# The mask and the query decay tables of a retention + two-layer FFN kernel made on the chip from small tables, with the second weight words loaded later and two decoding steps moved behind one sum

## The chip, the cores and the metric

One core of one Trainium2 chip runs the whole program. The metric is the device time of one execution in microseconds (us), median of three runs. The engines are TensorE (PE, its weight loads are PEld), VectorE (DVE), ScalarE (ACT), GpSimd (POOL) and SyncE (SP, which here only issues DMAs). Each takes its own instructions strictly in program order and waits where an operand, or a buffer that it will overwrite, is not free.

## The reference

Retention (attention with a decay per head and no softmax), then two feed-forward layers over the same 2304 tokens:

```python
scores = scale * np.matmul(q, k.transpose(0, 1, 3, 2))      # q, k, v: 4 x 8 x 576 x 64
gamma = 1.0 - 2.0 ** (-5.0 - np.arange(H, dtype=np.float32))
rel = pos[:, None] - pos[None, :]
Dmat = np.where(rel >= 0, gamma[:, None, None] ** rel[None, :, :], 0.0)
x = np.matmul(scores * Dmat[None], v)                       # -> 2304 x 512
h = x @ w_in;  x = np.maximum(0.01 * h, h) @ w_out          # 512 -> 2048 -> 512
h = x @ moe2_w_in;  h = np.maximum(h, 0.0);  return (h * h) @ moe2_w_out
```

The inputs q, k, v are float32. The weights are float64 and reach the chip as pairs of 32-bit words.

## The kernel before

**Retention** runs over 20 chunks (4 batches, each of four chunks of 128 tokens and one of 64; chunks 4, 9, 14 and 19 are the short ones). In the text chunk i has these steps: s_i (`scores`, L541) multiplies queries and keys of the chunk on PE; r_i (L544, L546) multiplies the scores by the mask on DVE; `decay` multiplies q (L555) and one half of k's heads (L559) by decay tables on POOL, `decay_rest` (L567) the other half of k's heads on ACT; out_i (L581, L590) forms the chunk's output on PE, which ACT copies out (L593); sums_i (L599) adds the chunk to the running state, which ACT copies (L603). The table `gq[0]` holds the query decays of the second chunk of a batch; those of later chunks are scaled copies of it (`make_gq`, L492). Scores go to two wide PSUM buffers by turns, so s_i needs r_(i-2) done. Loads are issued by SP in the order of the code: six buffers for q and k, four for the rows of k and v.

**Decoding.** Each weight pair of words ("raw") is turned into two float32r parts by steps on ACT and DVE. `steps_in` makes seven combinations of the first matrix (L153 on ACT, then L163 to L183 on DVE, L189 on ACT, L191 on DVE); `steps_out` does the second matrix (L153, L204, L206, L208, L210, L212 on DVE, L215 on ACT, L217, L220 on DVE). `run(n, limit)` writes the next n steps at the place in program order where it is called. The first pair of words lands in a part of `ysb[2]`, all later ones in one staging buffer, `raw`.

**The layers** hold eight groups of four blocks of 128 hidden units (`g`), and in each group three parts of 768 tokens (`p`). `first` runs seven products (Strassen-like, L321) into two PSUM buffers `a` and `b` by turns: A11, A12, S2, S3, S1, A22, S4. Between them DVE forms sums; the one of this text is L390, which reads `a` after product S1 and has to be done before product S4 writes `a` again. `second` (L425) has two halves t = 0, 1; in layer 0 each half fills four accumulators (e = 0 to 3), which share four PSUM banks with those of the other half, in layer 1 three accumulators take the four banks by turns. In group 0 ACT copies each finished accumulator out (L434). While group 0 of a layer works on a part, `operands` prepares the next part (L260 on ACT; L264, L274, L276, L279, L285 on DVE). `pace` is called between the products and accumulators with a running count `now`; `run` in it writes up to two decoding steps, except at counts 6 and 8 of each part's 15.

The order of every engine is the order in which the code is written; nothing reorders it.

Of the kernel before, what the change touches and what calls it, by code (L numbers as in the profile page):

```python
# [19 lines left out]
P = 128  # L20
# [32 lines left out]
@with_exitstack  # L53
def retention_ffn_kernel(ctx: ExitStack, tc: tile.TileContext, full, rows, half, halfv, w1, w2, const, mask, gk, out):

# [399 lines left out]
    class Retention:  # L455
# [27 lines left out]

        def load_gq(self):
            nc.sync.dma_start(self.gq[0].rearrange("p a t -> p (a t)"), const)

        def make_gq(self, c):

            if 1 < c <= FULL:
                to = self.gq[c - 1]  # L490
                for a in range(NP):
                    nc.scalar.activation(to[:, a], self.gq[0][:, a, : to.shape[2]], AF.Copy, scale=self.step[:, c - 2, a : a + 1])  # L492

        def load_mask(self):
            nc.sync.dma_start(self.mask.rearrange("p j a t -> p (j a t)"), mask)

# [136 lines left out]
    with tc.manual_schedule():  # L633
        with tc.tile_pool(name="att", bufs=1) as pool, tc.tile_pool(name="outputs", bufs=1, space=PSUM) as outputs:
            att.append(Retention(pool, outputs))
            ret = att[0]
            n = len(chunks)
            ret.load(0)
            weights.ahead()
            ret.load_mask()  # L640
            ret.load_gk()
            ret.load_rows(0)
            ret.load(1)
            ret.load_gq()
            ret.load(2)
# [4 lines left out]
            ret.open_table()  # L650
            ret.keep_warm(WARM[0])
            ret.scores(0)
            ret.decay(0)
            run(FIRST, GROUP)
            ret.decay_rest(0)
            scored = 1
            for i in range(n):
                if i + DEEP < n:
                    ret.load(i + DEEP)
                if i + ROWS < n:  # L660
                    ret.load_rows(i + ROWS)
                if i == 1 or weights.loads < GRP and weights.free:
                    weights.free = False
                    weights.ahead()
# [5 lines left out]
                ret.keep_warm(WARM[i + 1] if i + 1 < len(WARM) else 0)  # L670
                ret.output(i)
                ret.make_gq(i + 2)
                if i + 1 < n:
# [37 lines left out]
        for layer in range(2):  # L711
            for g in range(NG):
# [6 lines left out]
                def pace(now, ceiling):  # L719

                    into = min(1, (now - 15 * p) / (6 if busy[p] else 12 if p == NB - 1 else 15))
                    share = (0, *SHARE.get(i, (0.36, 0.71)), 1)
                    part = share[p] + (share[p + 1] - share[p]) * into
                    want = start + math.ceil((limit - start) * part)

                    while len(kept) > LAG:
                        store(*kept.pop(0))
                    while builds and now >= built[0] and build():
                        built[0] = max(built[0], now - 1) + SPACE
                    if not builds:  # L730
                        while kept:
                            store(*kept.pop(0))
                    weights.clock = whole * i + now
                    if now % 15 not in (6, 8):
                        run(min(2, max(want, start if now > 1 else 0) - done[0]), ceiling)
# [27 lines left out]
def constants():  # L763

    gamma = (1.0 - 2.0 ** (-5.0 - np.arange(H, dtype=np.float32))).astype(np.float64)
    scale = 1 / np.sqrt(D)
    row, col = np.arange(P)[:, None], np.arange(C)[None, :]
    gq = gamma[row // D + 2 * (col // P)] ** (P + col % P) * scale
    pair = np.arange(NP)[None, :]
    step = [gamma[row // D + 2 * pair] ** (c * P) for c in range(1, FULL)]  # L770
    since = col % P - row
    mask = [np.where(since >= 0, gamma[2 * (col // P) + j] ** np.maximum(since, 0) * scale, 0) for j in range(2)]
    gk = gamma ** -(np.arange(FULL)[:, None] * P + row[:, :, None]).astype(np.float64)
    return [a.astype(np.float32) for a in (gq, np.concatenate(mask, axis=1), np.concatenate([gk.reshape(P, -1), *step], axis=1))]

# [46 lines left out]
```

## Time and profile before

| | |
|---|---|
| median of 3 runs | 825.92 us (825.62 to 826.03) |
| the profiled execution | 826.09 us, its span 824.3 us |
| granted TensorE clock | 1.00 of full speed over the span |
| PE busy | 810.1 us, 98% of the span |
| DVE busy | 594.0 us, 72% |
| ACT busy | 352.3 us, 43% |
| POOL busy | 37.5 us, 5%, all of it in the first 75 us |

The times in the sections below are microseconds from the start of the span; the execution's own time is 1.8 us longer than the span. "Idle" is time of an engine just before an instruction; the name behind "<-" is what ended it.

### The profile page before, as it was taken

The page shows a single profiled execution, that of the slowest core. Times are in us where ns is not written, and L with a number is a line of the kernel's source. Part 1 is how long each engine was busy: PE and PEld are TensorE (multiplying, and loading weights), DVE is VectorE, ACT ScalarE, POOL GpSimd, SP SyncE. Part 2 cuts the span into 40 slices and gives each one's busy share as a digit, 9 for nine tenths or more (in the row PEclk, how much of TensorE's full clock was granted, in tenths as well). Part 3 has the DMA queues.
Part 4 walks back from the last instruction along what each step waited for, and adds up shares of the span by engine and source line. Part 5 has one row for each costly group of instructions (what it writes and reads, how often), then busy time and mean ns, then how long its engine had stood idle before and what let it go on. Part 6 is the DMA issues. An engine that isn't in the chain of part 4 may idle for free.

```text
span 824.3 us, 12698 instructions
## 1 busy us (share of the span) xinstructions
PE 810.1 (98%) x5216; PEld 765.3 (93%) x5216; DVE 594.0 (72%) x734; ACT 352.3 (43%) x511; POOL 37.5 (5%) x36
## 2 busy tenths in 40 slices
PE   7999999999999999999999999999999999999998
PEld 7788999999999999999999888998998998998996
DVE  5798887766665766667668989878876877853644
ACT  4777666453342452352444556443323333311211
POOL 3563000000000000000000000000000000000000
PEclk9999999999999999999999999999999999999999
DMA  9997549874773665665715437964864845744712
GB/s 349 395 362 295 219 148 361 342 286 134 293 254 139 246 253 178 259 228 193 269 52 230 165 155 270 397 234 150 312 224 155 308 173 205 263 171 179 289 51 76
DMA packets 45130, 190.91 MB, mean 232 GB/s; under 512 B 5136, under 2 KB 6160, under 8 KB 45072
## 3 DMA queue, kind: packets, MB, share of 16 engines
q1 hardware_dynamic: 44784, 189.31, 61.8%
q8 instruction: 41, 0.67, 0.3%
q10 hardware_dynamic: 288, 0.79, 0.3%
q14 instruction: 17, 0.14, 0.0%
HBM read 152.33 MB, written 37.75 MB: 231 GB/s over the span
## 4 chain that ended last, share of the span: by engine, by line
PE 86%; DVE 5%; DMA 4%; ACT 2%; issue 1%; SPq 0%; ACTq 0%; DVEq 0%
PE yps L425 45%; PE a L321 22%; PE b L321 16%; DMA kv<-in_rows 3%; DMA raw<-in_w 1%; PE ops L590 1%; PE scps L541 1%; DMA ysb<-in_w 1%; ACT sf L153 1%; PE ops L581 1%; DVE ilo L191 0%; ACT t L333 0%; PE sums L599 0%; DVE t L376 0%; DVE sf L167 0%
## 5 line engine op out<-in xcount | busy, mean ns | idle before, releaser
L321 PE MATMUL a<-x,ihi 128*128 128x384 f32 x768 | 195.9, 335 | 2.3 <-DVE t L390 2.3
L321 PE MATMUL b<-x,ihi 128*128 128x384 f32 x568 | 144.3, 334 | 0.0
L321 PEld LDWEIGHTS a<-x,ihi 128*128 128x128 f32 x768 | 138.6, 188 | 4.6 <-DVE t L390 3.5
L425 PE MATMUL yps<-ghi,ohi 128*128 128x384 f32 x384 | 128.6, 335 | 0.4 <-ACT ysb L434 0.4
L321 PE MATMUL a<-x,ilo 128*128 128x384 f32 x384 | 128.5, 335 | 0.0
L425 PE MATMUL yps<-glo,ohi 128*128 128x384 f32 x384 | 128.3, 334 | 0.0
L425 PE MATMUL yps<-ghi,olo 128*128 128x384 f32 x384 | 128.3, 334 | 0.0
L362 DVE TENSOR_TENSOR glo<-t,ghi 128x768 fp32r<-128x768 f32 x96 | 91.7, 955 | 45.9 <-ACT ghi L357 45.4
L436 DVE TENSOR_TENSOR ysb<-yps,ysb 128x384 f32<-128x384 f32 (+1 forms) x126 | 75.9, 610 | 61.9 <-PE yps L425 61.6
L425 PE MATMUL yps<-ohi,glo 128*128 128x512 f32 x288 | 112.3, 390 | 0.0
L425 PE MATMUL yps<-olo,ghi 128*128 128x512 f32 x288 | 112.3, 390 | 0.0
L425 PE MATMUL yps<-ohi,ghi 128*128 128x512 f32 x288 | 112.0, 389 | 0.0
L357 ACT ACTIVATE ghi<-t 128x768 fp32r<-128x768 f32 x96 | 81.1, 845 | 68.2 <-DVE t L335 54.8
L350 ACT ACTIVATE s<-a 128x768 f32<-128x768 f32 x47 | 38.2, 813 | 154.7 <-PE a L321 154.7
L321 PEld LDWEIGHTS b<-x,ihi 128*128 128x128 f32 x568 | 102.5, 188 | 0.4 <-ACT s L350 0.3
L321 PE MATMUL b<-x,ilo 128*128 128x384 f32 x284 | 94.9, 334 | 0.0
L425 PEld LDWEIGHTS yps<-ghi,ohi 128*128 128x128 f32 x384 | 72.1, 188 | 1.3 <-ACT ysb L434 0.7
L425 PEld LDWEIGHTS yps<-ghi,olo 128*128 128x128 f32 x384 | 72.1, 188 | 0.0
L425 PEld LDWEIGHTS yps<-glo,ohi 128*128 128x128 f32 x384 | 72.1, 188 | 0.0
L321 PEld LDWEIGHTS a<-x,ilo 128*128 128x128 f32 x384 | 72.1, 188 | 0.0
L425 PEld LDWEIGHTS yps<-ohi,glo 128*128 128x128 f32 x288 | 54.0, 188 | 11.3
L425 PEld LDWEIGHTS yps<-olo,ghi 128*128 128x128 f32 x288 | 54.0, 188 | 11.0
(77 smaller groups left out, 981.4 us busy)
## 6 DMA issues: line engine op xcount, KB each, us to landing
x<-x SPq DMA_DIRECT2D x168, 768.0 KB, 6.0
raw<-in_w SPq DMA_DIRECT2D x62, 512.0 KB, 5.7
kv<-in_rows SPq DMA_DIRECT2D x16, 512.0 KB, 6.6
out<-ysb SPq DMA_DIRECT2D x18, 256.0 KB, 2.0
q<-in_full SPq DMA_DIRECT2D x16, 256.0 KB, 6.5
kt<-in_full SPq DMA_DIRECT2D x15, 256.0 KB, 6.0
kv<-in_halfv SPq DMA_DIRECT2D x4, 256.0 KB, 6.5
ysb<-in_w ACTq DMA_DIRECT2D x1, 512.0 KB, 6.5
```

What stands on the lines that cost most here:

```text
L153: nc.scalar.activation(f32(a), f32(raw[:, :, 1]), AF.Abs)
L321: nc.tensor.matmul(ps[:, u, :HT], a[:, w, s], x[:, b, k], start=(start and k == 0 and i == 0), stop=(k == 1 and i == 2), skip_group_check= ...
L350: nc.scalar.activation(t, ps[:, :, :HT], AF.Copy)
L357: nc.scalar.activation(h, t, AF.Copy)
L362: nc.vector.tensor_tensor(l, t, f32(gs[key][0]), sub)
L425: nc.tensor.matmul(acc, a, b, start=(j == u == i == 0), stop=(j == 1 and u == NU - 1 and i == 2))
L436: nc.vector.tensor_tensor(y, acc, y, add)
L541: nc.tensor.matmul(o, k[s, c], q[s, c], start=True, stop=True, skip_group_check=True)
L581: nc.tensor.matmul(o, self.state[s, a], q[s, a * n : (a + 1) * n], start=(p == 0), stop=False, skip_group_check=True)
L590: nc.tensor.matmul(o, kv[f, 1, s], r, start=(c == 0 and p == 0), stop=(p == NP - 2), skip_group_check=True)
```

## The change

Three things change.

**Tables.** The mask (128 x 1024 float32, 512 KB) and the first query table (128 x 512, 256 KB) are no longer loaded. A table of 8 x 1792 float32 (57 KB: per head the powers of gamma, going down along the keys and up along the queries, and a selector of heads) and a causal table of 128 x 128 zeros and ones (64 KB) are loaded instead, into a part of `ysb[1]`. Two PE products over 8 rows give the powers of all heads; DVE multiplies them by the causal table into the mask. A third product gives the query table, which ACT copies out of PSUM. That product's PSUM bank is the one in which `keep_warm` writes.

**Loads.** The second pair of words is issued in iteration 2 of the chunk loop instead of iteration 1. The scores of chunk 1 and their mask are written directly behind out_0, ahead of two decoding steps.

**Pace.** At count 4 of a part no decoding steps are written where a group 0 works on a part that prepares the next one, except for the very first: that is part 1 of layer 0, and parts 0 and 1 of layer 1. The steps come later in the same part.

```diff
+        def load_tables(self):
+            t = ysb[1].rearrange("p (i n) -> p i n", i=2 * NK)
+            self.powers, self.cause = t[:H, :5].rearrange("p i n -> p (i n)")[:, : 2 * P + 3 * C], t[:, 5, :P]
+            nc.sync.dma_start(self.powers, const)
+        def load_cause(self):
+            nc.sync.dma_start(self.cause, cause)
+        def make_mask(self):
+            left, right = self.powers[:, :P], self.powers[:, 2 * P :]
+            ps = wide(1, "mps")
+            for j in range(2):
+                nc.tensor.matmul(ps[:, j], left, right[:, j * C : (j + 1) * C], start=True, stop=True)
+            heads = [t.rearrange("p j a t -> p (j a) t") for t in (self.mask, ps.rearrange("p j (a t) -> p j a t", t=P))]
+            nc.vector.tensor_tensor(*heads, self.cause.unsqueeze(1).to_broadcast([P, H, P]), mul)
+        def first_gq(self):
+            ps = bank("gps", 3)
+            nc.tensor.matmul(ps, self.powers[:, P : 2 * P], self.powers[:, 2 * P + 2 * C :], start=True, stop=True)
+            nc.scalar.activation(self.gq[0].rearrange("p a t -> p (a t)"), ps, AF.Copy)
...
             ret.load(0)
+            ret.load_tables()
             weights.ahead()
-            ret.load_mask()
+            ret.load_cause()
             ret.load_gk()
             ret.load_rows(0)
             ret.load(1)
-            ret.load_gq()
             ret.load(2)
...
             ret.keep_warm(WARM[0])
+            ret.make_mask()
             ret.scores(0)
+            ret.first_gq()
             ret.decay(0)
...
-                if i == 1 or weights.loads < GRP and weights.free:
+                if i == 2 or weights.loads < GRP and weights.free:
...
                 ret.output(i)
+                if i == 0:
+                    ret.scores(1)
+                    ret.decay(1)
+                    scored = 2
                 ret.make_gq(i + 2)
...
-                    if now % 15 not in (6, 8):
+                    if now % 15 not in ((4, 6, 8) if g == 0 and busy[p] and i + p else (6, 8)):
```

At the start of ACT's program the query table's copy comes in (gq_80 is the first query table, gps the PSUM bank, ysb_68 holds the first words). Before:

```order
L475 ACTIVATE ysb_66<-ysb_66 128x1
L153 ACTIVATE sf<-ysb_68 128x1024
L567 ACTIVATE kv<-kv,gk 128x64 x4
L593 ACTIVATE ysb_66<-ops 128x4x128
L603 ACTIVATE state<-sums 128x256
```

And in the changed kernel, whose lines are numbered higher (L585 is the old L567, L611 the old L593, L621 the old L603):

```order
L475 ACTIVATE ysb_66<-ysb_66 128x1
L506 ACTIVATE gq_80<-gps 128x512
L153 ACTIVATE sf<-ysb_68 128x1024
L585 ACTIVATE kv<-kv,gk 128x64 x4
L611 ACTIVATE ysb_66<-ops 128x4x128
```

The copy stands ahead of everything that ACT does for the decoding and the first chunk.

At the start of DVE's program the mask is made, and the product r_1 of chunk 1 moves ahead of L169 and L172. Before:

```order
L544 TENSOR_TENSOR r<-scps,mask 128x1024
L163 TENSOR_SCALAR sf<-sf 128x1024
L165 TENSOR_SCALAR sf<-sf 128x1024
L167 SCALAR_TENSOR_TENSOR sf<-ysb_68,sf 128x1024
L169 TENSOR_SCALAR sf<-sf 128x1024
L172 SCALAR_TENSOR_TENSOR sf<-ysb_68,sf 128x1024
L544 TENSOR_TENSOR r<-scps,mask 128x1024 x2
```

And after (L562 is the old L544):

```order
L500 TENSOR_TENSOR mask<-mps,ysb_67 128x1024
L562 TENSOR_TENSOR r<-scps,mask 128x1024
L163 TENSOR_SCALAR sf<-sf 128x1024
L165 TENSOR_SCALAR sf<-sf 128x1024
L167 SCALAR_TENSOR_TENSOR sf<-ysb_68,sf 128x1024
L562 TENSOR_TENSOR r<-scps,mask 128x1024
L169 TENSOR_SCALAR sf<-sf 128x1024
L172 SCALAR_TENSOR_TENSOR sf<-ysb_68,sf 128x1024
```

One instruction is added and one has moved up by two.

In part 1 of layer 0's group 0 DVE has these rows before (L390 is the sum, L204 to L212 the decoding, L264 and L274 the preparing of part 2):

```order
L204 TENSOR_SCALAR raw<-raw 128x1024
L206 TENSOR_SCALAR sf<-sf 128x1024
L390 TENSOR_TENSOR t<-a,s 128x768
L208 SCALAR_TENSOR_TENSOR sf<-raw 128x1024
L210 TENSOR_SCALAR sf<-sf 128x1024
L395 TENSOR_TENSOR t<-b,s 128x768
L362 TENSOR_TENSOR glo<-t,ghi 128x768 x3
L264 TENSOR_TENSOR x<-ysb_68,x 128x768
L212 SCALAR_TENSOR_TENSOR sf<-raw,sf 128x1024
```

And after:

```order
L390 TENSOR_TENSOR t<-a,s 128x768
L204 TENSOR_SCALAR raw<-raw 128x1024
L206 TENSOR_SCALAR sf<-sf 128x1024
L395 TENSOR_TENSOR t<-b,s 128x768
L362 TENSOR_TENSOR glo<-t,ghi 128x768 x3
L264 TENSOR_TENSOR x<-ysb_68,x 128x768
L208 SCALAR_TENSOR_TENSOR sf<-raw 128x1024
L210 TENSOR_SCALAR sf<-sf 128x1024
L264 TENSOR_TENSOR x<-ysb_68,x 128x768
L274 TENSOR_TENSOR ysb_68<-ysb_68 128x2x384
L212 SCALAR_TENSOR_TENSOR sf<-raw,sf 128x1024
```

L390 has moved ahead of two steps, and L212 behind four instructions more.

ACT at the same place, before (L215 reads what L212 wrote, L434 empties the accumulators):

```order
L260 ACTIVATE x<-ysb_68 128x768 x2
L215 ACTIVATE ohi<-sf 128x1024
L434 ACTIVATE ysb_67<-yps 128x384 x4
L260 ACTIVATE x<-t_1580 128x768
```

And after:

```order
L260 ACTIVATE x<-ysb_68 128x768 x2
L434 ACTIVATE ysb_67<-yps 128x384
L215 ACTIVATE ohi<-sf 128x1024
L434 ACTIVATE ysb_67<-yps 128x384 x3
L260 ACTIVATE x<-t_1585 128x768
```

One of the four copies has moved ahead of L215; three stand behind it as before.

## Rows read from the trace of the kernel before

**Rows 1.** Windows: us, busy us of each engine, clock, DMA share, GB/s.

```profile
0.00:43.50 43.50, 36.35 (x642) 32.23 (x642) 30.18 (x34) 26.62 (x75) 19.74 (x22) 1.00 0.99 374
43.50:75.00 31.50, 30.85 (x576) 27.41 (x577) 30.01 (x32) 23.74 (x63) 17.72 (x15) 1.00 0.94 348
```

**Rows 2.** PE's waits: us in total, times, longest us.

```profile
PE a L321 <- DVE t L390: 2.3, 2, 1.1
...
PE yps L425 <- ACT ysb L434: 0.4, 1, 0.4
```

**Rows 3.** The chain that ended last: start us, us, what.

```profile
31.51 0.70 DVE sf L163
```

**Rows 4.** DMA issues: size each, us from issue to landing (first q, a raw).

```profile
q<-in_full SPq DMA_DIRECT2D x1, 256.0 KB, 3.5
raw<-in_w SPq DMA_DIRECT2D x1, 512.0 KB, 7.3
```

**Rows 5.** Timeline of the first 15 us: start us, us, engine, line, what.

```profile
6.47 1.38 PE L482 MATMUL cold<-cold 128*128 128x128 f32 x10
...
7.67 1.13 ACT L153 ACTIVATE sf<-ysb 128x1024 f32<-128x1024 f32 x1 [4.53 <-DMA ysb<-in_w]
...
9.68 1.06 ACT L567 ACTIVATE kv<-kv,gk 128x64 f32<-128x64 f32 x4 [0.88 <-DMA kv<-in_rows]
...
11.28 1.16 PE L541 MATMUL scps<-q,kt 64*128 64x128 f32 x16
...
13.18 2.17 DVE L172 SCALAR_TENSOR_TENSOR sf<-ysb,sf 128x1024 f32<-128x1024 uint32 x1
...
13.44 1.16 PE L541 MATMUL scps<-q,kt 64*128 64x128 f32 x16 [1.00 <-DMA kt<-in_full]
```

**Rows 6.** Timeline of 15 to 32 us.

```profile
15.27 2.34 DVE L544 TENSOR_TENSOR r<-scps,mask 128x1024 f32<-128x1024 f32 x2
...
17.67 1.96 SPq L136 DMA_DIRECT2D raw<-in_w  x2
...
19.83 1.22 DVE L544 TENSOR_TENSOR r<-scps,mask 128x1024 f32<-128x1024 f32 x1
...
21.20 1.77 PE L541 MATMUL scps<-q,kt 64*64 64x64 f32 x32
...
26.85 0.38 ACT L593 ACTIVATE ysb<-ops 128x256 f32<-128x256 f32 x1
...
29.37 1.06 ACT L567 ACTIVATE kv<-kv,gk 128x64 f32<-128x64 f32 x4 [2.14 <-DMA kv<-in_rows]
```

**Rows 7.** Timeline of layer 0, group 0, parts 1 and 2.

```profile
113.97 0.95 DVE L390 TENSOR_TENSOR t<-a,s 128x768 f32<-128x768 f32 x1
...
114.97 0.62 PE L321 MATMUL a<-x,ihi 128*128 128x384 f32 x2 [1.12 <-DVE t L390]
...
115.97 0.69 DVE L210 TENSOR_SCALAR sf<-sf 128x1024 uint32<-128x1024 uint32 x1
...
122.63 1.22 DVE L212 SCALAR_TENSOR_TENSOR sf<-raw,sf 128x1024 uint32<-128x1024 uint32 x1
...
123.88 1.06 ACT L215 ACTIVATE ohi<-sf 128x1024 fp32r<-128x1024 f32 x1 [1.55 <-DVE sf L212]
124.85 1.61 ACT L434 ACTIVATE ysb<-yps 128x384 f32<-128x384 f32 x4
...
160.64 1.23 DVE L172 SCALAR_TENSOR_TENSOR sf<-raw,sf 128x1024 f32<-128x1024 uint32 x1
```

**Rows 8.** Timeline of layer 1, group 0, parts 1 and 2.

```profile
491.16 0.95 DVE L390 TENSOR_TENSOR t<-a,s 128x768 f32<-128x768 f32 x1
...
500.52 0.95 DVE L264 TENSOR_TENSOR x<-ysb,x 128x768 fp32r<-128x768 f32 x1
...
500.99 0.58 ACT L434 ACTIVATE ysb<-yps 128x512 f32<-128x512 f32 x1
...
522.33 0.95 DVE L390 TENSOR_TENSOR t<-a,s 128x768 f32<-128x768 f32 x1
```

More of the change, by code (lines that the diff above doesn't have):

```diff
@@ L53, in retention_ffn_kernel @@
 @with_exitstack
-def retention_ffn_kernel(ctx: ExitStack, tc: tile.TileContext, full, rows, half, halfv, w1, w2, const, mask, gk, out):
+def retention_ffn_kernel(ctx: ExitStack, tc: tile.TileContext, full, rows, half, halfv, w1, w2, const, cause, gk, out):
     nc = tc.nc
@@ L492, in make_gq @@
                     nc.scalar.activation(to[:, a], self.gq[0][:, a, : to.shape[2]], AF.Copy, scale=self.step[:, c - 2, a : a + 1])
-        def load_mask(self):
-            nc.sync.dma_start(self.mask.rearrange("p j a t -> p (j a t)"), mask)
         def make_last(self):
@@ L766, in constants @@
     scale = 1 / np.sqrt(D)
-    row, col = np.arange(P)[:, None], np.arange(C)[None, :]
-    gq = gamma[row // D + 2 * (col // P)] ** (P + col % P) * scale
+    row = np.arange(P)[:, None]
+    head, to = np.arange(H)[:, None], np.arange(C)[None, :]
+    left = gamma[head] ** -np.arange(P)[None, :].astype(np.float64)
+    mine = head % 2 == np.arange(P)[None, :] // D
+    right = [np.where(head == 2 * (to // P) + j, gamma[head] ** (to % P) * scale, 0) for j in range(2)]
+    right.append(np.where(head // 2 == to // P, gamma[head] ** (P + to % P) * scale, 0))
+    cause = np.arange(P)[None, :] >= row
     pair = np.arange(NP)[None, :]
     step = [gamma[row // D + 2 * pair] ** (c * P) for c in range(1, FULL)]
-    since = col % P - row
-    mask = [np.where(since >= 0, gamma[2 * (col // P) + j] ** np.maximum(since, 0) * scale, 0) for j in range(2)]
     gk = gamma ** -(np.arange(FULL)[:, None] * P + row[:, :, None]).astype(np.float64)
-    return [a.astype(np.float32) for a in (gq, np.concatenate(mask, axis=1), np.concatenate([gk.reshape(P, -1), *step], axis=1))]
+    return [a.astype(np.float32) for a in (np.concatenate([left, mine, *right], axis=1), cause, np.concatenate([gk.reshape(P, -1), *step], axis=1))]
 def kernel(q, k, v, moe_w_in, moe_w_out, moe2_w_in, moe2_w_out):
@@ L803, in weights @@
         return np.stack([a, w_out.reshape(NF, P, DM)], axis=1).view(np.int64)
-    const, mask, gk = constants()
+    const, cause, gk = constants()
     arrays = {
@@ L808 @@
         "w1": weights(heads_turned(moe_w_in), moe_w_out), "w2": weights(moe2_w_in, moe2_w_out),
-        "const": const, "mask": mask, "gk": gk,
+        "const": const, "cause": cause, "gk": gk,
     }
```

2 lines of the change are left out of this document (removed).

## The prediction, as it was made before the changed kernel ran

> **What bounds the kernel now.** I read the windows first, to see where PE is idle at all. In the first 43.5 us it is busy for 36.35, while the DMA engines are at 0.99; from 43.5 to 75 us it is busy for 30.85 of 31.50, and DVE for 30.01 [rows 1]. PE's waits, read next, show what is left behind that: two waits for L390, 2.3 us together and at most 1.1 each, and one of 0.4 for an ACT copy [rows 2]. So this change can gain in two ways: by bringing everything behind the retention's start forward, or by removing the two waits. For the first the chain that ended last says what has to come earlier: DVE's L163 at 31.51, the start of decoding the second words, from which DVE's work leads without a break into PE's dense stretch [rows 1, 3]. L163 waits for ACT, and ACT had waited 2.14 us for the rows of chunk 5, a load [rows 6]. That is a start limited by loads, with ACT and DVE close behind.
>
> **The loads.** Out go 512 + 256 KB, in come 57 + 64 KB: 647 KB less, at 374 GB/s [rows 1] 1.75 us; I use 1.65, since the rate is a little higher once the queue is full. The second words are 1024 KB, and three loads of chunk 7 and 5 with the same sum now pass them: those come another 2.6 us earlier. The rows of chunk 5 landed at 29.3 and land at 25.0. The words, issued from 17.67 in two pieces of 1.96 us together and landing 7.3 later [rows 4, 6], came at 26.6 and come at 26.6 - 1.65 + 2.6 = 27.6. So with nothing else in the way L163 could start 2.6 us earlier (words 27.6, L153 1.14, then DVE at 28.9): the most that the start can give.
>
> **What stands in the way: ACT's new first instruction.** The powers stand second on SP, behind a load issued at 0.74 that lands 3.5 later [rows 4], and 57 KB take 0.15 us: I take 4.85. It can't be below 4.25, and not much above 7.6, when the first words, issued behind it, were there for L153 [rows 5]. The three table products are plain float32, 512 columns each. The nearest row is the warming product of the same type, five of 128 columns in 1.38 us, so 0.21 to 0.28 each [rows 5]; four times the columns give 0.85 to 1.1. I take 0.85, since a long product hides its start. Two run before s_0, which takes 1.16 [rows 5], and one behind it: with 0.1 to start the first and 0.15 for the hand-over that is 4.85 + 1.8 + 1.16 + 1.0 = 8.8. The copy on ACT, 0.58 like an L434 of the same size [rows 8], ends at 9.4, and L153, which started at 7.67, starts there: 1.75 later. The copy also holds the bank in which the warming products write, so out_0 starts 1 us later. The mask itself costs nothing: causal table landed at 7.2, product 1.22 like r_3 [rows 6], r_0 done at 9.6, while DVE has nothing else until L153's 10.55.
>
> I follow the delay as differences. The scaling of k for chunk 0 on ACT: 9.68 to 10.55 [rows 5]. Sums_0 needs it, s_1 stands behind: 11.28 to 12.3. s_2 had waited 1.00 us for its keys [rows 5] and no longer does: 13.44 to 13.4, so PE has caught up. DVE has not: r_1 starts when s_1 ends, 13.6, then L169 (0.69, the kind of L210, [rows 7]), L172 (2.17, [rows 5]) and r_2 end at 18.9, where they ended at 15.27 + 2.34 = 17.6 [rows 6]. Moving r_1 ahead gives PE out_1 sooner, but the sum of DVE's work up to r_2 is the same. r_3 ends 1.3 later as well, at 22.35. s_5 overwrites its PSUM buffer: it was the last 1.1 us of a row that ended at 22.97 [rows 6] and now ends at 23.5, 0.55 to 0.6 later. Out_3, s_6, out_4 follow on PE, and ACT's copy of out_4, 26.85 before, starts at 27.5 and ends at 27.9 [rows 6]. There the chain meets the loads: ACT had then waited until 29.37 for chunk 5 [rows 6], whose rows are now there. So ACT goes on 1.4 us sooner, L153 finds its words (27.6 against 29.0), and allowing 0.1 for the hand-overs L163 starts at 30.2. **Term 1: -1.3 us.** Behind it DVE's chain and then PE are dense [rows 1, 3] and move as a whole.
>
> Its bounds. L172 took 2.17 us while POOL scaled q; in layer 0, without POOL, the same form takes 1.23 [rows 5, 7]. Were it that fast here, r_3 would be 0.9 sooner, and the term about -2.1. [...] Upwards, every microsecond by which the powers or products are late moves L153 by one: powers at 7.6 make the term +1.45. [...]
>
> **The pace, layer 0.** L390 ran at 113.97 behind two steps of 0.60 each. Without them it runs at 112.76 and ends at 113.7, and PE, free at 114.97 - 1.12 = 113.85, doesn't wait [rows 7]: -1.12. But the steps come back. DVE's next instructions are all 1.75 us sooner (L395: 116.57 to 114.83); yet L212 now stands behind L208 (1.14), L210 (0.60), a second L264 and L274 (0.87 each), 3.48 in all. It starts at 122.63 - 1.75 + 3.48 = 124.36 and ends at 125.6, where it ended at 123.85 [rows 7]. ACT's L215 waits for it, and behind L215 stand the copies of the second to fourth accumulator. Before, all four came at 124.85, 0.1 before PE asked for the first bank [rows 7]. Now the first is done early, and the second ends at 125.6 + 0.97 + 0.48 = 127.05. PE, 1.12 sooner, begins its second half at 124.25 and wants the second bank at 125.3: it waits 1.75. **Term 2: -1.12 + 1.75 = +0.65 us.** That PE does wait for such a copy is seen once, 0.4 us, in the part behind [rows 2]. The bounds: -1.1 with no wait behind, +1.0 with L212 a further 0.35 late.
>
> **The pace, layer 1.** Part 0 had no wait. In part 1 L390 moves from 491.16 [rows 8] by the same 1.14 and 0.60 to 489.42, and PE's wait of 1.1 is gone [rows 2]. L215 goes behind the preparing here too: the first L264, at 500.52 before [rows 8], comes at 499.4, L212 runs behind it from 500.25 to 501.45, L215 takes 0.97, the first copy (500.99 before, 0.58 long, [rows 8]) ends at 503.0. PE needs that bank for the second accumulator of its second half, seven runs of six products, 1.36 us each, behind a start at 493.2: 502.75. A wait of 0.3. In part 2, where nothing is left out, L206 now stands ahead of four L264 and waits for ACT; L390 (522.33 before, [rows 8]) comes at 522.0, while PE is 0.8 sooner: a wait of 0.4 that was not there. **Term 3: -1.14 + 0.3 + 0.4 = -0.4 us**, bounds -1.1 and 0.
>
> **Sum.** -1.3 + 0.65 - 0.4 = -1.05 us against the profiled execution's 826.09, 0.2 above the median. On the median of 825.92 that is **824.9 us**. I take 0.2% (1.65 us) as what a measurement of this kernel tells from no change, so this is inside.
>
> **Rivals.** (a) The two waits for L390 go and nothing takes their place: -1.3 - 1.12 - 1.14 = -3.6, 822.4 us. For it: ACT and DVE are idle for over a quarter of the span. Against: in the rows L215 comes right when L212 ends, and three copies stand behind it in order. (b) The start gains more, DVE being less held: -2.1, at the most -2.6, so with terms 2 and 3 about 824.0. (c) The tables come late and ACT's copy holds up decoding, since it stands ahead of L153: powers at 7.6, with the first words, give 1.45 + 0.65 - 0.4 = +1.7, 827.6 us. That is also the point from which it decides: it takes 2.7 us in all, from the load or from products slower than the 0.85 taken. For it: a load ahead of the words is new, and nothing here shows its time. Against: loads of one queue landed in the order of their issue. (d) The loads were not the limit, since ACT and DVE are as full: term 1 is 0, 826.2 us.
>
> **Chances.** The forecast 50% (its own range 823.9 to 825.9), (a) 13%, (b) 15%, (c) 12%, (d) 10%. Faster by over 0.2%: all of (a), over half of (b), a fifth of the forecast's spread: 32%. Slower by over 0.2%: half of (c) and a little of the rest, 7%. Within: 61%. The range from 822.6 to 827.0 leaves out half of (a) and the outer half of (c).
>
> **What would show it.** Right: ACT's first copy ends near 9.4 and L153 follows at once; L163 of the second words at about 30.2, not waiting for its load; PE's dense stretch from about 42.2; no wait of PE for L390 in part 1, but one of over 1 us for L434 ten microseconds later, with ACT idle ahead of L215; shorter waits in layer 1, one of them in part 2. Wrong: powers landing after 5.5; s_5 not waiting for r_3; L163 still waiting for a DMA; PE running through the second half of part 1.

## The result, and the profile after

The changed kernel takes 831.07 us (median of six executions, 829.11 to 833.90) against 825.77 of the kernel before: 1.0064 times as long, 95% interval 1.0054 to 1.0074. It is slower, by 5.3 us, where 824.9 was forecast. The profiled execution is the slowest of the six (833.90); how it got 7.8 us behind the one before is read below, and the scatter has a cause of its own that the runs show.

Where does the time go? Both kernels run ACT's L357 96 times in the same order, so the start of each can be set against that of its counterpart, stage by stage:

| L357 of before at | 77.0 | 108.9 | 118.4 | 141.7 | 173.3 | 485.5 | 494.2 | 524.3 to the end |
|---|---|---|---|---|---|---|---|---|
| later in the changed kernel by | 6.08 | 6.06 | 4.65 | 8.67 | 7.88 | 7.95 | 6.71 | 7.79 |

So 6.1 us are lost in the start (forecast: 1.3 gained). Part 1 of layer 0 gains 1.4 and then loses 4.0, part 2 gives 0.8 back, and layer 1 gains 0.2 in all. The windows of the start, as in [rows 1]:

```profile
0.00:43.50 43.50, 38.31 (x548) 32.06 (x550) 27.93 (x29) 23.81 (x68) 18.81 (x20) 0.88 0.91 319
43.50:75.00 31.50, 29.57 (x583) 26.07 (x580) 31.40 (x33) 21.93 (x61) 17.91 (x16) 1.00 0.91 326
```

DVE has done 27.9 us of work by 43.5 instead of 30.2, and after that it has no idle time left (31.40 of 31.50); the DMA engines, full before, are at 0.91. The timeline says where DVE's work was held up:

```profile
6.11 1.98 PE L498 MATMUL mps<-ysb 8*128 8x512 f32 x4 [1.28 <-DMA ysb<-in_const]
8.02 1.96 PE L559 MATMUL scps<-q,kt 64*128 64x128 f32 x16
8.68 1.23 DVE L500 TENSOR_TENSOR mask<-mps,ysb 128x1024 f32<-128x1024 f32 x1 [7.67 <-DMA ysb<-in_cause]
9.92 2.07 PE L505 MATMUL gps<-ysb 8*128 8x512 f32 x2
12.02 0.60 ACT L506 ACTIVATE gq<-gps 128x512 f32<-128x512 f32 x1 [8.86 <-PE gps L505]
12.52 1.12 ACT L153 ACTIVATE sf<-ysb 128x1024 f32<-128x1024 f32 x1
12.67 2.50 PE L482 MATMUL cold<-cold 128*128 128x128 f32 x10 [0.69 <-ACT gq L506]
13.67 0.69 DVE L163 TENSOR_SCALAR sf<-sf 128x1024 f32<-128x1024 f32 x1 [2.42 <-ACT sf L153]
15.11 1.98 PE L608 MATMUL ops<-r,kv 128*64 128x128 f32 x16
17.87 2.31 PE L559 MATMUL scps<-q,kt 64*128 64x128 f32 x32
19.33 1.23 DVE L562 TENSOR_TENSOR r<-scps,mask 128x1024 f32<-128x1024 f32 x1 [2.98 <-PE scps L559]
...
36.46 1.03 DVE L163 TENSOR_SCALAR sf<-sf 128x1024 f32<-128x1024 f32 x1
```

ACT's first copy and L153 behind it stand as the order said, but at 12.0 and 12.5, not at 8.8 and 9.4. DVE then waits twice, 2.42 us for L153 and 2.98 for s_1, with L169 and L172 standing behind r_1. The warming products take 2.50 us for ten rows that took 1.38 before [rows 5]. The windows show the clock (the column before the DMA share):

```profile
6.00:8.00 2.00, 1.89 (x4) 0.66 (x4) 0.00 (x0) 0.00 (x0) 0.00 (x0) 1.00 1.05 382
8.00:10.00 2.00, 2.00 (x18) 1.75 (x17) 1.23 (x1) 0.00 (x0) 0.00 (x0) 0.55 1.02 390
16.00:18.00 2.00, 2.00 (x30) 1.88 (x26) 0.35 (x1) 0.60 (x1) 0.00 (x0) 0.50 1.08 387
18.00:20.00 2.00, 2.00 (x32) 1.98 (x32) 0.67 (x1) 1.99 (x8) 0.57 (x1) 0.89 1.02 395
...
134.00:136.00 2.00, 2.00 (x9) 2.00 (x8) 1.69 (x3) 2.00 (x4) 0.00 (x0) 0.62 0.86 270
136.00:138.00 2.00, 2.00 (x8) 2.00 (x8) 2.00 (x3) 1.25 (x2) 0.00 (x0) 0.53 0.92 313
```

From 8.2 to 18.4 us and again from 134.5 to 137.9 TensorE's granted clock is 0.50, the lower level in what follows, against 1.00, the upper one. Ahead of the first fall it had waited 1.28 us and then run products over 8 rows; ahead of the second it had waited 1.94 us. PE's waits, as in [rows 2], and that second place, as in [rows 7]:

```profile
PE yps L425 <- ACT ysb L434: 2.4, 2, 1.9
...
PE a L321 <- DVE t L390: 0.3, 1, 0.3
```

```profile
130.76 1.22 DVE L212 SCALAR_TENSOR_TENSOR sf<-raw,sf 128x1024 uint32<-128x1024 uint32 x1
...
132.01 1.06 ACT L215 ACTIVATE ohi<-sf 128x1024 fp32r<-128x1024 f32 x1 [4.08 <-DVE sf L212]
132.98 1.23 ACT L434 ACTIVATE ysb<-yps 128x384 f32<-128x384 f32 x3
...
133.50 0.44 PE L425 MATMUL yps<-ghi,ohi 128*128 128x384 f32 x1 [1.94 <-ACT ysb L434]
```

That wait is the forecast one: ACT idle for 4.08 us ahead of L215, three copies behind it, PE 1.94 us without a bank. The clock behind it had no price in the forecast.

### The profile page after: what moved, and what is told of

It reads as the page before. It is cut to its first block, busy times and chain, and to the rows that moved or that the text cites. A ratio compares the mean times of both kernels' runs of the same rounds, so it can differ in the third digit from the quotient of the medians.

```text
span 832.1 us, 12715 instructions
## 1 busy us (share of the span) xinstructions
PE 817.9 (98%) x5222; PEld 770.2 (93%) x5222; DVE 598.7 (72%) x735; ACT 352.8 (42%) x512; POOL 36.7 (4%) x36
## 4 chain that ended last, share of the span: by engine, by line
PE 82%; DVE 10%; ACT 3%; issue 2%; DMA 2%; SPq 0%; DVEq 0%; ACTq 0%
PE yps L425 43%; PE a L321 21%; PE b L321 15%; DVE r L562 1%; DVE x L264 1%; DMA raw<-in_w 1%; PE ops L608 1%; PE scps L559 1%; ACT sf L153 1%; DVE sf L212 1%; DMA ysb<-in_const 1%; ACT t L333 1%; DVE sf L208 1%; ACT ghi L357 1%; DVE sf L210 1%
## 5 line engine op out<-in xcount | busy, mean ns | idle before, releaser
L425 PE MATMUL yps<-ghi,ohi 128*128 128x384 f32 x384 | 129.3, 337 | 2.0 <-ACT ysb L434 1.9
L425 PE MATMUL yps<-ghi,olo 128*128 128x384 f32 x384 | 129.0, 336 | 0.0
L425 PE MATMUL yps<-glo,ohi 128*128 128x384 f32 x384 | 128.9, 336 | 0.0
L425 PE MATMUL yps<-ohi,ghi 128*128 128x512 f32 x288 | 112.1, 389 | 0.4 <-ACT ysb L434 0.4
L425 PE MATMUL yps<-ohi,glo 128*128 128x512 f32 x288 | 112.3, 390 | 0.0
L425 PE MATMUL yps<-olo,ghi 128*128 128x512 f32 x288 | 112.3, 390 | 0.0
L357 ACT ACTIVATE ghi<-t 128x768 fp32r<-128x768 f32 x96 | 81.1, 845 | 73.2 <-DVE t L335 59.7
L425 PEld LDWEIGHTS yps<-ghi,ohi 128*128 128x128 f32 x384 | 72.7, 189 | 2.9 <-ACT ysb L434 2.3
L425 PEld LDWEIGHTS yps<-glo,ohi 128*128 128x128 f32 x384 | 72.6, 189 | 0.0
L425 PEld LDWEIGHTS yps<-ghi,olo 128*128 128x128 f32 x384 | 72.5, 189 | 0.0
L425 PEld LDWEIGHTS yps<-ohi,ghi 128*128 128x128 f32 x288 | 54.1, 188 | 11.8 <-ACT ysb L434 0.9
L425 PEld LDWEIGHTS yps<-ohi,glo 128*128 128x128 f32 x288 | 54.0, 188 | 11.3
```

The source lines that it names most:

```text
L357: nc.scalar.activation(h, t, AF.Copy)
L425: nc.tensor.matmul(acc, a, b, start=(j == u == i == 0), stop=(j == 1 and u == NU - 1 and i == 2))
```

## The experiments

Fifteen kernels besides the changed one, each with five to twelve executions next to 17 to 27 of the kernel before. "Late at 77" and "at 529" are L357's delay against the kernel before in the one execution that was profiled; that one can lie at the edge of its run (in e10 it is the slowest of eleven, in e14 the fastest of five).

| run | median, us | ratio to before (95%) | late at 77 | at 529 |
|---|---|---|---|---|
| changed kernel | 831.07 | 1.0064 (1.0054 to 1.0074) | 6.08 | 7.80 |
| e1_pace_back | 830.77 | 1.0067 (1.0045 to 1.0088) | 6.59 | 6.73 |
| e2_pace_only | 826.57 | 1.0010 (1.0001 to 1.0018) | 0.25 | 0.40 |
| e3_warm13 | 830.09 | 1.0046 (1.0028 to 1.0065) | 3.91 | 4.02 |
| e4_warm_8rows | 826.16 | 0.9998 (0.9990 to 1.0007) | -0.08 | 0.16 |
| e5_gq_late | 829.34 | 1.0038 (1.0026 to 1.0050) | 3.26 | 3.43 |
| e6_no_early_scores | 831.78 | 1.0074 (1.0061 to 1.0086) | 3.39 | 5.17 |
| e7_s0_first | 831.73 | 1.0075 (1.0058 to 1.0092) | 6.03 | 7.85 |
| e8_three_moves | 829.41 | 1.0037 (1.0025 to 1.0050) | 3.10 | 3.33 |
| e8w_warm11 | 827.68 | 1.0019 (1.0010 to 1.0027) | 0.14 | 1.87 |
| e9_catch_up | 826.36 | 1.0005 (0.9996 to 1.0013) | 0.18 | 0.85 |
| e10_words_later | 825.86 | 1.0001 (0.9992 to 1.0009) | 1.36 | 1.35 |
| e11_probe_load | 826.48 | 1.0003 (0.9994 to 1.0013) | 0.65 | 0.87 |
| e12_tables_alone | 826.88 | 1.0016 (1.0007 to 1.0026) | 0.98 | 0.82 |
| e13_copies_first | 828.12 | 1.0024 (1.0015 to 1.0034) | -0.16 | 1.83 |
| e14_both | 829.40 | 1.0039 (1.0027 to 1.0051) | 0.75 | 2.23 |

### The two halves of the change: e1 and e2

e1 is the changed kernel, e2 the kernel before, with this line turned about:

```diff
-if now % 15 not in ((4, 6, 8) if g == 0 and busy[p] and i + p else (6, 8)):
+if now % 15 not in (6, 8):
```

> The changed kernel with the pace of before (the exception at count 4 taken out again), so tables, load order and early scores alone. Theory: the loss of the start is the tables'. Set side by side, the same instructions of the changed kernel's trace run 6.1 us later than before's from 77 to 109 us, and the clock is at its lower level from 8.2 to 18.4 us; so this kernel's profile has the same fall, the same 6 us behind it, PE's two waits for L390 (1.1 us each) back, and no lower clock after 20 us: 829 to 832 us. Rival: the fall of the clock early on is worth little and the pace is the loss, then the median is within 1 us of 825.8.

> The kernel before with the new pace alone. Theory: the wait of 1.9 us for the copy L434 in the second half of part 1 of layer 0 comes of the pace, and it is this wait that lowers the clock behind it (3.4 us at the lower level in the changed kernel, 1.7 us lost). With the wait for L390 gone (1.1) and 0.8 back in part 2, this gives +1.5 to +2 us: 827.3 to 827.8, both seen in the profile. Rival one (as the prediction had it): a wait of 1.75 and no lower clock, and so 826.1. Rival two: the pace alone gains its two waits for L390, 823.6.

The start costs 4.7 us in the medians (830.77 less 826.03) and the pace 0.5 (826.57 less 826.03); together 5.3, the whole loss, though e1's interval alone reaches from 3.7 to 7.3 us. e1 came as expected in time, e2 did not: in its profile the wait came, the lower clock behind it did not. PE's waits in e2:

```profile
PE yps L425 <- ACT ysb L434: 2.3, 2, 1.9
```

Over the profiles that carry the new pace unmended the two cases stand cleanly apart: between 118.4 and 141.7 L357 falls back by 2.43 or 2.44 in e2, e3, e5 and e8, where the clock stays at 1.00 there, and by 3.97 to 4.01 in the changed kernel, e6, e7 and e8w, where it falls. On PE itself the products L425 of part 1 take 16.8 us from the first to the last before, 18.9 to 19.1 in those four and 20.6 to 20.7 in the others. So the wait costs 2.1 to 2.4 and the lower clock, in half of the profiles, another 1.55 or so: part of the scatter. The executions without a profile fit this: e2's eleven times fall into two groups, six from 825.94 to 826.57 and five from 827.43 to 828.03, 1.4 us apart on average (mean granted clock 0.998 to 1.000 and 0.997 to 0.998). The pace's 0.5 in the median is thus a mixture, 0.2 in the one group and 1.6 in the other.

e1 expected the fall of the clock as in the changed kernel, and its clock row reads 1.00 throughout. But the products have the durations of the lower level from the first of them, 3.77 us for what took 1.98, and for ten rows of warming products the same 2.50 as the changed kernel at 0.50:

```profile
5.97 3.77 PE L498 MATMUL mps<-ysb 8*128 8x512 f32 x4 [1.13 <-DMA ysb<-in_const]
9.68 2.08 PE L559 MATMUL scps<-q,kt 64*128 64x128 f32 x16
...
14.44 2.50 PE L482 MATMUL cold<-cold 128*128 128x128 f32 x10 [0.69 <-ACT gq L506]
```

```profile
8.00:10.00 2.00, 2.00 (x5) 0.50 (x5) 0.22 (x1) 0.00 (x0) 0.00 (x0) 1.00 1.02 387
```

So the durations have to be read beside the clock column near the start: in e1, e5 and e8 it reads 1.00 in every row from 6 to 24 us, and what is said of the lower level there is read from the durations.

### The clock: e3, e4, e8 and e8w

e3 is the changed kernel with `WARM = 13, 5, 3` for `8, 5, 3`; e4 the kernel before with

```diff
+                rows = H if n == WARM[1] else P
-                    nc.tensor.matmul(ps[:, :P], self.cold, self.cold, start=True, stop=True)
+                    nc.tensor.matmul(ps[:, :P], self.cold[:rows], self.cold[:rows], start=True, stop=True)
```

> The changed kernel with 13 instead of 8 warming products at the start, which fill PE's wait of 1.28 us for the powers (4.83 to 6.11 us); the table products start where they did. Theory A: PE's idle time ahead of them lowers the clock. Then the clock stays at its upper level, the 10 us at the lower one (5 us lost) are won back, and the start is late by about 1 us instead of 6: 826 us. Theory B: the products over 8 rows don't keep the clock up. Then it falls again at about 8 to 10 us and the time stays at 829 to 832 us.

> The kernel before, with its five warming products behind s_0 over 8 rows of the zero tile instead of 128; they take as long, and nothing depends on their values. PE then has 1.4 us of them and 1.9 us of waiting, as before. Theory A (only idle time counts): clock 1.00 throughout, 825.8 us. Theory B (products over 8 rows count for little): the clock falls between 8 and 12 us and the time goes up by 2 to 5 us.

e8 moves three things in the changed kernel, e8w has `WARM = 11, 5, 3` besides:

```diff
-            ret.make_mask()
-            ret.first_gq()
...
+            if i == 0:
+                self.make_mask()
             if n == P:
                 nc.vector.tensor_tensor(t, ps, self.mask, mul)
...
                 ret.output(i)
                 if i == 0:
-                    ret.scores(1)
-                    ret.decay(1)
-                    scored = 2
+                    ret.first_gq()
```

> The changed kernel's tables and loads with all three moves at once: s_0 ahead of the table products, the query table behind the sums of chunk 0, s_1 and r_1 back behind L169 and L172. Pace as in the changed kernel. Theory: each delay of DVE's first instructions is passed on, since DVE has no idle time left from 20 to 75 us in the changed kernel; what stays is the mask itself (1.2 us of DVE) and the two products ahead of it. DVE's L163 then starts at 11.4 instead of 13.7 (9.46 before), without the later wait of 2.98 for s_1: the rows from 77 us on come 0 to 2 us after before's, 826.5 to 828.5 us with the pace. Rival: the load limit of before is the end of it and the freed loads show: 1 us earlier than before, 825.

> The same with 11 instead of 8 warming products, which fill PE's wait for the first keys (4.83 to 5.9 us). Theory: where the products behind it run at the lower clock (3.8 instead of 1.9 us for the two mask products) that is 2 us of DVE's start; with the wait filled they run at the upper one in the profile, and the time is 1 to 2 us under the version without. Rival: the clock falls all the same, some microseconds later: no difference.

e8 and e8w differ in three warming products alone, which fill PE's wait of 0.66 us for the first keys:

```profile
5.49 2.08 PE L559 MATMUL scps<-q,kt 64*128 64x128 f32 x16 [0.66 <-DMA kt<-in_full]
7.50 3.77 PE L498 MATMUL mps<-ysb 8*128 8x512 f32 x4
```

```profile
5.92 1.16 PE L559 MATMUL scps<-q,kt 64*128 64x128 f32 x16
7.01 1.98 PE L498 MATMUL mps<-ysb 8*128 8x512 f32 x4
```

The first pair is e8, the second e8w. 3.0 us at 77 in the two profiles, and 1.7 in the medians, come of that: e8w's expectation held, and e8 with its 829.41 missed the 826.5 to 828.5 that had left the clock out. With the wait filled (e3, e8w, e12, e14) the mask's products took 1.98 to 2.01 us in four profiles of four; unfilled, 1.98 twice (the changed kernel, e6), 2.94 once (e7) and 3.77 or 3.78 three times (e1, e5, e8), and in all six the products from 8.5 to 13 us ran at the lower level (the column at 0.50 in the changed kernel, e6 and e7, the durations 1.6 to 1.9 times those of the upper level in e1, e5 and e8). Which it is changes from execution to execution: e3 went from 826.67 us, at a mean granted clock of 1.000, to 833.52, at 0.994. So theory A holds as far as the start of the stretch goes. It isn't all: in three of the four profiles with the wait filled the clock fell all the same, a little later. In e3 it fell at 10.4, during the last table product, and e3's 830.09 us lie where theory B put them; in e14 it fell at 11.0, and in e8w at 9.1:

```profile
8.00:10.00 2.00, 2.00 (x9) 1.24 (x8) 0.97 (x1) 1.32 (x2) 0.13 (x1) 0.79 1.02 391
10.00:12.00 2.00, 1.68 (x10) 1.39 (x11) 1.97 (x3) 0.88 (x4) 0.48 (x1) 0.50 1.05 389
```

In e4, where the five warming products run over 8 rows, the clock was at its lower level from 7.5 to 14.3 in the profile, and its mean was below 1.000 in ten executions of ten (0.995 to 0.998), against 13 of 26 of the kernel before. That is what theory B had, but e4's time is that of the kernel before, as in theory A. The lower clock cost nothing there: PE waits for the rows of chunk 0 at that point (2.8 us in e4). e2 and e13, which start as the kernel before does, show the same: they were at the lower level from 9.9 to 13.4 and from 11.1 to 14.5, and at 77 they are 0.25 late and 0.16 early. That it does cost in the changed kernel is shown by e8 and e8w; the reason given here, that the mask, the query table and s_1 now stand ahead of DVE's and ACT's first work, is read from the order of the queues. What decides between a fall and none in one execution stays open.

The first products of all have a slow pace too, with the column at 1.00: the first sixteen rows of warming products take 3.78 us in the kernels before and after, 0.24 each, where the ten behind s_0 take 0.14 each before [rows 5]. The moment at which it ends differs between profiles: s_0, right behind the first sixteen, took 1.77 us in the kernel before and 1.16 in e9, whose start is the same.

### Order in the start: e5, e6, e7

e5 moves only `first_gq` behind `output(0)`, e6 only takes out the early `scores(1)`, e7 only moves `make_mask` behind s_0's products (the three edits of e8, one at a time).

> The changed kernel with the query table's product and its copy moved behind out_0 and the sums of chunk 0 (nothing reads the table before q_1). Theory: what costs is ACT's copy ahead of L153: in the changed kernel's trace the gps product ends at 12.0, and L153 starts at 12.5 with its words there since about 8, L163 at 13.7 instead of 9.5, and the warming products and out_0 wait for the same copy. Without it L153 starts at about 8, L163 at 9.2, and instructions from 77 us on are 2 to 4 us earlier than in the changed kernel (which had +6.1): 827 to 829 us. Rival: r_1, written ahead of L169 and L172, holds DVE until s_1 in any case; then DVE's later work moves by under 1 us.

> The changed kernel with s_1, r_1 and q_1 written where they stood before (behind the two decoding steps). Theory: DVE is the engine that the start is short of (9.9 of 10 us busy from 20 to 30, 31.4 of 31.5 from 43.5 to 75), and its wait of 2.98 us ahead of r_1, with L169 and L172 (2.3 us) behind it, is lost for good. With the two ahead of r_1 the wait shrinks to under 1 us and everything behind comes 2 to 2.3 us earlier: 828 to 829 us. Rival: the early product lets PE go on sooner and so pays for itself; then the time stays or grows.

> The changed kernel with s_0 ahead of the table products on PE, which need not wait for the powers then; the mask is still made ahead of r_0. Theory A: the products' place costs: PE works through from s_0 (keys at 5.6), the mask products end at about 9.5 and the gps product at 10.5, so ACT's copy comes 1.5 us earlier, and the rest with it: +4.5 instead of +6.1 from 77 us on, and no lower clock or a shorter stretch of it. Theory B: products over 8 rows lower the clock wherever they stand; then the clock falls at 8 to 10 us as well, s_0 alone being quicker, and the time stays.

One row of e5 and one of e6:

```profile
8.49 1.12 ACT L153 ACTIVATE sf<-ysb 128x1024 f32<-128x1024 f32 x1 [5.34 <-DMA ysb<-in_w]
```

```profile
19.04 2.36 DVE L562 TENSOR_TENSOR r<-scps,mask 128x1024 f32<-128x1024 f32 x2 [1.27 <-PE scps L559]
```

e5: L153 starts at 8.49 instead of 12.52, now waiting for its words and not for the copy. 2.8 us are won at 77 in the profile, and 1.7 in the medians. The profile's 2.8 can't be put down to the copy alone, since the clock went another way there (by the durations lower from the first product to 13.6, not from 8.2 to 18.4). The medians show that the copy ahead of L153 is a real cost. e6: in its profile, whose clock went as in the changed kernel's, DVE's wait for s_1 shrank from 2.98 to 1.27 and 2.7 us were won at 77; but its median is 0.7 above the changed kernel's, not 2 to 3 below. Over executions the early scores are not shown to cost anything: inconclusive. e7: no gain at all, a miss for theory A; the table products now took 2.94 and 1.91 us, as theory B had it. e7 doesn't separate the two, though, for PE still waited 1.18 us, now for the first keys. e8, with all three moves, has the median of e5, with one (829.41 and 829.34): the other two add nothing that shows.

### What the loads were worth: e10 and e11

e10 is the kernel before with `i == 2` for `i == 1` in the condition for the second words. e11 is the kernel before with an extra load ahead of the first words, into a place that nothing reads:

```diff
+            t = ysb[1].rearrange("p (i n) -> p i n", i=2 * NK)
+            t = t[:H, :5].rearrange("p i n -> p (i n)")[:, : 2 * P + 3 * C]
+            nc.sync.dma_start(t, mask.rearrange("(a b) n -> a (b n)", b=2)[:H, : 2 * P + 3 * C])
```

> The kernel before with the second words issued one iteration later, nothing else. By the prediction's working the words come 2.6 us later than 26.6 and three loads as much earlier: L163 of the second words, at 31.51 before, waits for them until 30.7 at the latest or for DVE's own work; so a gain of up to 0.8 us: 825.0 to 825.9 us. Rival: the words then land after they are wanted, L163 comes later than 31.51 and the time grows by up to 1 us.

> The kernel before with one load more, 8 rows of 7168 bytes (57 KB) from another table, in the place of the powers' load; nothing reads it. In the changed kernel's trace such a load was issued at 1.2 and there at 6.0, and the first keys landed at 5.6 instead of 4.4 us, with 123 to 246 GB/s moved from 4.2 to 5.7 us. Theory: the load over 8 rows holds back the loads behind it by 1.2 us: keys at 5.6, s_0 at 5.7 to 5.9 instead of 4.76; the time grows by 0 to 1.2 us, as far as PE has no slack. Rival: it costs its bytes only (0.15 us).

In e10 L163 did come earlier, by 1.16 us, and the time didn't move (825.86 against 825.89). DVE gives most of it back within 10 us:

```profile
30.35 0.69 DVE L163 TENSOR_SCALAR sf<-sf 128x1024 f32<-128x1024 f32 x1 [0.86 <-ACT sf L153]
...
33.04 2.18 DVE L167 SCALAR_TENSOR_TENSOR sf<-raw,sf 128x1024 uint32<-128x1024 uint32 x1
35.15 1.21 DVE L544 TENSOR_TENSOR r<-scps,mask 128x1024 f32<-128x1024 f32 x1
36.29 1.20 DVE L169 TENSOR_SCALAR sf<-sf 128x1024 uint32<-128x1024 uint32 x1
```

Before, L163 started at 31.51 [rows 3], L167 took 1.52 and L169 0.68:

```profile
34.51 1.52 DVE L167 SCALAR_TENSOR_TENSOR sf<-raw,sf 128x1024 uint32<-128x1024 uint32 x1
...
37.08 0.68 DVE L169 TENSOR_SCALAR sf<-sf 128x1024 uint32<-128x1024 uint32 x1
```

In e10 POOL is busy beside them (its q from 32.42 for 1.73 us, k from 34.10 for 1.60, q from 35.66 for 1.28), but in the kernel before it is too (k from 34.10 for 0.84, q from 34.91 for 2.27, k from 37.13 for 1.10). What makes the two longer in e10 is not shown; no run here takes POOL's work away. At 43 us DVE is 0.35 ahead of the kernel before. Behind that this profile is no measure of the edit: it is the slowest of its eleven executions (827.41), with the clock at the lower level from 43.6 to 47.1.

e11: the keys came at 4.5 us, not 5.6, and the time is that of before within the interval (its median is 0.6 above). Theory missed. The load does slow those beside it (287 GB/s from 4 to 5 us where the kernel before moves 406), and the rows of chunk 0 land later, but the 1.2 us by which the keys are late in the changed kernel are not its doing alone. What else holds them back stays open.

### The waits in a row: e9, e13, and e12, e14 for the sum

e9 lets the kernel before catch up directly behind the count that is skipped; e13 also puts L215 behind the four copies of layer 0's part 1. Its condition holds in parts 0 and 1 of layer 1 too, where it moves decoding steps in the same way:

```diff
-if now % 15 not in (6, 8):
-    run(min(2, ...
+if now % 15 not in ((4, 6, 8) if g == 0 and busy[p] and i + p else (6, 8)):          # e9
+    run(min(4 if now % 15 == 5 and g == 0 and busy[p] and i + p else 2, ...
+swap = g == 0 and busy[p] and i + p                                                 # e13
+if now % 15 not in ((4, 6, 8, 9.5, 10, 10.5) if swap else (6, 8)):
+    run(min({5: 4, 9: 1}.get(now % 15, 2) if swap else 2, ...
```

> The kernel before with the new pace, and up to four decoding steps instead of two at count 5, behind the skipped count 4. DVE's order then differs from before's only in L390 (one of them in each of three parts), which moves ahead of two steps; L212, L215 and the copies L434 stand where they stood. Theory: the waits for L390 (1.12 and 1.14) are real, and what took the gain was only L212's move behind the preparing: both waits go, no wait of over 0.5 us for L434 and no lower clock in part 1, 823.5 to 824 us. Rival: PE waits for another instruction that those steps now delay (L395, or L335 in layer 1), and the time stays within 1 us of 825.8.

> The kernel before with the catch-up pace, and L215 behind the four copies L434 instead of ahead of them in part 1 of layer 0 (one step at count 9, none at 9.5 to 10.5). Theory: the two waits were in series. The copies no longer wait for L212 and L215, PE waits for neither L390 nor L434 in part 1, the 1.1 us stay gained, and 0.4 in part 2 with them if its copy doesn't stand behind L215 there: 824.4 to 825.0 us; layer 1 as in the catch-up run, where a wait of 0.5 for L434 took the place. Rival: another wait follows (for L362's low parts, or for weights that L215 makes too late), and the time stays within 0.4 us of before.

In e9 both waits for L390 are gone, and nothing is gained (826.36 against 825.96, 1.0005 with an interval that holds 1). PE's waits from 100 us on, of e9 and then of e13:

```profile
PE yps L425 <- ACT ysb L434: 1.9, 3, 0.8
PE yps L425 <- DVE glo L362: 0.3, 1, 0.3
```

```profile
PE yps L425 <- ACT ysb L434: 3.3, 2, 2.1
```

In part 1 PE is 1.1 us early and finds the copies where they always were, behind L212 and L215: 0.8 is waited there, 0.6 in part 2, 0.5 in layer 1. With L215 out of the way (e13) part 1 runs without a wait and L357 is 1.04 early at 141.7. Then, in part 2 and in layer 1:

```profile
155.77 1.12 ACT L153 ACTIVATE sf<-raw 128x1024 f32<-128x1024 f32 x1 [3.94 <-DMA raw<-in_w]
...
157.32 0.45 PE L425 MATMUL yps<-ghi,ohi 128*128 128x384 f32 x1 [1.18 <-ACT ysb L434]
...
505.25 1.18 ACT L153 ACTIVATE sf<-raw 128x1024 f32<-128x1024 f32 x1 [3.42 <-DVE olo L220]
...
506.96 0.50 PE L425 MATMUL yps<-ohi,ghi 128*128 128x512 f32 x1 [2.13 <-ACT ysb L434]
```

In part 2 the copies stand behind L153, and that waits for its load until 155.8; in the kernel before it started at 156.04, also behind that load, and PE's wait of 0.4 [rows 2] is this one:

```profile
156.04 1.12 ACT L153 ACTIVATE sf<-raw 128x1024 f32<-128x1024 f32 x1 [3.17 <-DMA raw<-in_w]
```

Most of what PE wins in part 1 it waits here, 1.18 instead of 0.4: at 173.3 L357 is 0.39 early, of 1.04. Another 0.5 goes between there and 485.5, in e9 and e14 alike, without a wait of PE that the profile shows; this stays open. In layer 1 L153 waits for L220, which the edit made late, and 1.6 more are lost. The rival had the mechanism, another wait behind the first, but not its size: 828.12 us are 2.2 over the kernel before, not within 0.4.

e12 is e8w with the pace of before, e14 e8w with e13's pace.

> The tables in the best order found (s_0 first, query table behind the sums, s_1 and r_1 in their old place, 11 warming products, second words later) with the pace of before. With the new pace its rows at 77 us came 0.14 us after before's, and the end 1.9 us later in that profile. Theory: the pace made all of that, and the tables neither gain nor cost: 825.9 to 826.3 us, PE's two waits for L390 back. Rival one: the 647 KB not loaded show at last, 825.0 or less. Rival two: the clock falls again in the start in most executions and the median is over 827.

> Both: the tables in the best order and the pace with L215 behind the copies. Theory: nothing that the one moves is near what the other moves (under 77 us, and 109 to 140 and 484 to 530 us), so the two differences add up: e13's gain plus e12's difference, 824.5 to 825.5 us. Rival: the clock in the start spreads the times, as in the versions before, and the median stays at 826 or above.

e12: 0.9 us slower than before, with interval; the theory's 825.9 to 826.3 is missed by little, and the freed loads don't show. e14: the sum of e12 and e13 by their medians is 3.1, measured 3.4; they add up, as losses. No version tried beats the kernel before.

By the medians, in the order in which the parts were taken out, the loss of the changed kernel comes apart like this: 1.7 for the copy ahead of L153 (831.07 to e5's 829.34), nothing for the two other moves (e8, 829.41), 1.7 for PE's unfilled wait and the clock behind it (e8w, 827.68), 0.8 for the pace (e12, 826.88), and 0.9 that stays in e12 over its kernel before. The 0.9 have no test. In e12's profile DVE makes the mask in 1.23 us ahead of r_0, and its first L163 starts at 11.95, not at 9.46, of which 0.98 are left at 77.

## Why the prediction was wrong

**Term 1, forecast -1.3, measured +6.1 at 77 us in the profile and +4.7 in the medians (e1): the step that failed.** Three parts of it fell.

- *Durations.* "I take 0.85" and the rest of PE's chain came from rows at the upper clock. The powers landed at 6.1, not 4.85, and PE ran dry at 4.83. From 8.2 us on the products ran at the lower level: 2.07 for the query table's, 1.96 for s_0, 2.50 for the warming. ACT's copy started at 12.0 instead of 8.8: 1.2 of the 3.2 us are the powers' load, 2.0 the products. The pair e8, e8w shows the clock, e5 the copy; no run brings the powers alone earlier, so the load's share has no price of its own. Two of the prices were low even so. The 1.16 taken for s_0 are those of later chunks [rows 5], while s_0 itself took 1.77 in the kernel before (below), and 1.16 to 1.98 in later runs with the same start; and 0.85 was the lower end of 0.85 to 1.1, where a table product takes 0.99 at the upper level (two in 1.98). The start that a long product hides is seen in the warming products of the kernel before, three in 0.94 us and five in 1.38: 0.22 for each further one and 0.28 once. L172, priced at 2.17 as beside POOL, took 1.52 at 21.29 us in the changed kernel, with POOL at work the whole time (k from 20.66 for 1.06, q from 21.69 for 2.26), so no run shows that POOL's work makes it 2.17.

```profile
4.76 1.77 PE L541 MATMUL scps<-q,kt 64*128 64x128 f32 x16
```

- *"PE has caught up. DVE has not."* The delay was expected to stop at waits for loads. L153 came 4.85 us late in place of 1.75, more than those waits could take in, and then DVE waited for PE: 2.98 us ahead of r_1. "The sum of DVE's work up to r_2 is the same" was true and beside the point, for the wait of 2.98 is no work. L163 of the second words started at 36.46, forecast 30.2.
- *"A start limited by loads."* Read off the DMA share of 0.99 and one chain [rows 1, 6]. The rate behind its 1.65 us, 392 GB/s, is that of the trace, 396 from 4 to 43.5 us. e10 brings those loads forward and L163 with them, and no time is won; e12 leaves out the 647 KB in the best order found, and is 0.9 slower than before. DVE is as full as the loads from 43.5 us on [rows 1], and two of its instructions took longer in e10. The 1.3 was not there to be won; on this point rival (d), given 10%, was right.

Rival (c) had the right mechanism, tables late and ACT's copy holding up L153, from the load or from slower products. Its +1.45 was too small: it priced a late load alone and not PE's clock. L153 came 3.1 us later than forecast, which by the prediction's own rule, one for one, makes the term +1.8; the rest of the 6.1 came behind L153, the wait of 2.98 first.

**Term 2, forecast +0.65, measured +1.8 in the profile after, +0.2 in e2.** The wait for L390 went and one of 1.94 (forecast 1.75) came for L434, through L212, L215 and the copies as written. The lower clock behind such a wait was missing from the sum: 1.55 us in half of the profiles. So was part 2, which gives 0.8 back in both profiles. In e2, without the lower clock, these errors nearly cancel; that its 0.2 is near the forecast is in part luck.

**Term 3, forecast -0.4, measured -0.2.** Both small waits came: 0.4 for L434 in part 1 (forecast 0.3), 0.3 for L390 in part 2 (forecast 0.4).

Of the signs listed, ACT's order, the wait of over 1 us for L434 with ACT idle ahead of L215, and the small waits of layer 1 were right. L163 at 30.2 was not (36.46). "Powers landing after 5.5" was named as a sign that the forecast is wrong, and it came.

## What to carry to other kernels

A product put in front of the first real work of TensorE is priced at both levels of its clock (the mask's two took 1.98 to 2.01 us in six profiles, 3.77 or 3.78 in three), and what PE waits for ahead of it is priced too (0.66 us in e8, 1.28 in the changed kernel); a wide scatter of the executions (829 to 834 here, 825.5 to 826.1 in the six of before beside them) can then be a sign of the clock, as in e3. A full DMA share (0.99 here) doesn't prove that loads limit a stretch, when the engine behind them is as full: bring the load forward alone and see (e10: L163 1.16 us earlier, 825.86 us against 825.89). A wait removed on the busiest engine gained only up to the next one in the queues of the others: here L390 (1.1 us), the copies behind L215 (0.8 in e9) and the copies behind a late load (1.18 in e13) stood in a row.

## What the runs showed that was not expected

- The clock column read 1.00 in the first microseconds while products took nearly twice the time that they took in other profiles (the mask's two 3.77 or 3.78 us in e1, e5 and e8, 1.98 in the changed kernel).
- One and the same wait of 1.9 us is followed by about 3.4 us at the lower clock in four profiles of eight, and not in the others.
- The load of 57 KB over 8 rows took 4.88 us from issue to landing, where 3.66 was forecast, and around it less is moved: from 4 to 6 us the changed kernel moves 197 and 262 GB/s at a DMA share of 1.18 and 0.86, the kernel before 406 and 410 at 1.02 and 1.01. What lowers the rate is not shown.
